# Two feed-forward layers: the first matrix of each in Strassen's 2x2 block scheme (7 block products instead of 8)

## Chip, cores and metric

One core of a Trainium2 chip runs one program. The metric is the device time of one execution in microseconds, as the median of runs. TensorE multiplies, VectorE and ScalarE read and write both SBUF and PSUM, GpSimd (POOL) works on SBUF, and SyncE (SP) issues the transfers.

## The reference

Attention over 2 x 8 heads of 576 tokens with 64 columns, with rotary tables, gives `x` of 1152 tokens and 512 columns. Then two feed-forward layers follow, and float32 accuracy is asked for:

```python
p = domain_probs / (domain_probs.sum(-1, keepdims=True) + 1e-09)
for e in range(4):                       # w1[e] 512 x 1024, w2[e] 1024 x 512, float32
    h = np.maximum(x @ w1[e], 0.0)
    out += p[:, e:e + 1] * (h @ w2[e])
x = out
h = x @ w_in                             # 512 x 2048, float64
g = np.maximum(0.01 * h, h)
return (g @ w_out).astype(np.float32)    # 2048 x 512, float64
```

## The kernel before

To keep float32 accuracy every operand of a matmul is held as two rounded halves, a high one and a low one, and each product is three matmuls (high x low, high x high, low x high).

The two layers are cut into 12 units of 512 hidden columns: units 0 to 7 are halves of the four experts, units 8 to 11 are quarters of the second layer. A unit's first matrix (`stage1`, L554 to L559, tile `ph`) works in blocks of 512, 384 and 256 tokens; for each block and each of four tiles of 128 hidden columns, 12 matmuls (four row chunks, three each) accumulate in one PSUM bank. Then ScalarE writes the rectified high half and VectorE the low half of `h` (L566, L570; in the second layer four steps, L578 to L584, the last on GpSimd). The second matrix (`stage2`, L586, tile `py`) takes 12 matmuls of 512 columns for each tile of 128 tokens, and VectorE adds them into `acc` (L605 or L609). For units 0 to 2 the first 512 tokens were already done during the attention part in half units (`half_1`, `half_2`), so these units have only the other 640 tokens.

The weights of a unit are loaded by SP into `raw` (8 buffers) and split into `w`, two buffers for each matrix: high half on GpSimd or ScalarE (L262, L260), low half `raw - high` on GpSimd (L519). The float64 weights of the second layer are narrowed as integers while they are needed, in eight steps a chunk (`split64`, L521 to L548). Between the layers every tile of `acc` is transposed on TensorE (L620) and split into `xT` (L623, L627).

The order on all engines is written out ahead by `Plan` (L77): each task has one or several possible engines with estimated durations, a rank, and the tasks that it must follow; a list scheduler gives each engine, whenever it is free in the plan, the ready task of lowest rank. What it writes is the program's fixed order, and each engine works its queue in that order.

```python
            t, e = best

            _, _, i, us = min((x for x in ready[e] if x[0] <= t), key=lambda x: (x[0], x[2]) if e == "DMA" else x[1:3])
            free[e] = t + us
            done[i] = e
```

Of the kernel before, what the change touches and what calls it, by code (L numbers as in the profile page):

```python
# [29 lines left out]
AHEAD = 3  # L30
FH = FU // 2
# [29 lines left out]
BLOCKS = [(0, 512), (512, 384), (896, 256)]  # L61
# [92 lines left out]
def attention_then_two_ffns(ctx, tc, xqk, vp, rope, dprob, w1, w2, w_in, w_out, out):  # L154
# [314 lines left out]
    RAW, W, ACC, HT, PH, PY, G, CV, TURN = ({} for _ in range(9))  # L469
    SEQ = [(u, b) for u in range(NU) for b in range(u < AHEAD, 3)]  # L470

    def unit_weights(u, which):
        if u < 2 * E:
            e, half = divmod(u, 2)
            a = (w1[e][:, half * FU:(half + 1) * FU], w2[e][half * FU:(half + 1) * FU, :])[which]
        else:
            j = u - 2 * E
            a = (w_in[:, j * FU:(j + 1) * FU], w_out[j * FU:(j + 1) * FU, :])[which].bitcast(I32)
        return a.rearrange("(c p) f -> p c f", p=P)

    def load_w(u, which, j, raw_p):

        src = unit_weights(u, which)
        if u < 2 * E:
            raw = RAW[u, which, j] = raw_p[0].tile([P, 2, raw_p[2]], F32, tag=raw_p[1], name=f"raw{u}_{which}_{j}")
            sp.dma_start(raw[:, :, :FU], src[:, 2 * j:2 * j + 2])
        else:
            raw = RAW[u, which, j] = raw_p[0].tile([P, FU, 2], I32, tag=raw_p[1], name=f"raw{u}_{which}_{j}")
            sp.dma_start(raw.rearrange("p f w -> p (f w)"), src[:, j])

    def w_place(u, which):
        if (u, which) not in W:
            pool_w = w2_p if which else w1_p
            W[u, which] = pool_w.tile([P, NC, 2, FU], F32R, tag=f"w{which}", name=f"w{which}_{u}")

    def add_split(plan, u, which, loaded, waits, rank, cv=None):

        res = []
        for c in range(NC):
            if u < 2 * E:  # L500

                hi = plan.add(lambda e, c=c: split_hi(e, u, which, c), [("POOL", 0.6, 0)] + [("ACT", 0.6, 0)] * (u == 0), loaded[c // 2:c // 2 + 1] + waits, rank + .1 * c)
                res.append(plan.add(lambda e, c=c: split_lo(e, u, which, c), [("POOL", 1.23, 0)] + [("DVE", 0.9, 0)] * (u == 0), [hi], rank + .1 * c))
                continue
            t = loaded[c:c + 1] + cv.new()
            for k, (e, us) in enumerate((("DVE", 0.85), ("DVE", 1.0), ("ACT", 0.65), ("ACT", 0.65), ("POOL", 1.4), ("DVE", 1.0), ("ACT", 0.62), ("POOL", 1.38))):
                t = [plan.add(lambda e, c=c, k=k: split64(u, which, c, k), [(e, us, 0)], t + (waits if k == 6 else []), rank + .1 * c)]
            cv.use(-1, t[0])
            res += t
        return res  # L510

    def split_hi(e, u, which, c):
        w_place(u, which)
        w, raw = W[u, which][:, c], RAW[u, which, c // 2][:, c % 2, :FU]
        rounded(e, w[:, 0], raw)

    def split_lo(e, u, which, c):
        w, raw = W[u, which][:, c], RAW[u, which, c // 2][:, c % 2, :FU]
        eng[e].tensor_tensor(out=w[:, 1], in0=raw, in1=f32(w[:, 0]), op=ALU.subtract)  # L519

    def split64(u, which, c, k):  # L521

        raw = RAW[u, which, c]
        low, high = raw[:, :, 0], raw[:, :, 1]
        if k == 0:
            CV[u, which, c] = [cv_p.tile([P, FU], d, tag=g, name=f"{g}{u}_{which}_{c}") for g, d in (("t", I32), ("r", I32), ("sq", F32))]
        t, r, sq = CV[u, which, c]
        if k == 0:

            dve.tensor_scalar(t, high, 3, 0x3FFFFFFF, op0=ALU.logical_shift_left, op1=ALU.bitwise_and)  # L530
        elif k == 1:
            dve.scalar_tensor_tensor(out=t, in0=high, scalar=-0x40000000, in1=t, op0=ALU.bitwise_and, op1=ALU.bitwise_or)  # L532
        elif k == 2:

            act.activation(r, low.bitcast(U32), AF.Copy, scale=2.0 ** -29)
        elif k == 3:
            act.activation(sq, high.bitcast(F32), AF.Square)
        elif k == 4:
            pool.tensor_tensor(out=t, in0=t, in1=r, op=ALU.add)  # L539
        elif k == 5:  # L540

            dve.scalar_tensor_tensor(out=f32(t), in0=sq, scalar=MIN_HIGH ** 2, in1=f32(t), op0=ALU.is_ge, op1=ALU.mult)
        elif k == 6:
            w_place(u, which)
            act.activation(W[u, which][:, c, 0], f32(t), AF.Copy)  # L545
        else:
            w = W[u, which][:, c]
            pool.tensor_tensor(out=w[:, 1], in0=f32(t), in1=f32(w[:, 0]), op=ALU.subtract)  # L548

    def h_place(k):  # L550
        u, blk = SEQ[k]
        HT[u, blk] = h_p.tile([P, 2, FU // P, 512], F32R, tag="h", name=f"h{u}_{blk}")

    def stage1(u, blk, f, ps, cs=range(NC)):  # L554
        w, x = W[u, 0], xT[blk]
        fs = slice(f * P, (f + 1) * P)
        for c in cs:
            for k, (l, r) in enumerate(((0, 1), (0, 0), (1, 0))):
                pe.matmul(ps, lhsT=w[:, c, l, fs], rhs=x[:, r, c], start=(c, k) == (0, 0), stop=(c, k) == (NC - 1, 2))  # L559

    def h_parts(u, blk, f):
        n = BLOCKS[blk][1]
        return HT[u, blk][:, 0, f, :n], HT[u, blk][:, 1, f, :n]

    def h_relu_hi(u, blk, f, ps):
        act.activation(h_parts(u, blk, f)[0], ps, AF.Relu)  # L566

    def h_relu_lo(u, blk, f, ps):
        hi, lo = h_parts(u, blk, f)
        dve.scalar_tensor_tensor(out=lo, in0=ps, scalar=0.0, in1=f32(hi), op0=ALU.max, op1=ALU.subtract)  # L570

    def h_leaky(u, blk, f, ps, k):
        hi, lo = h_parts(u, blk, f)
        if k == 0:
            G[u, blk, f] = g_p.tile([P, 512], F32, tag="g", name=f"g{u}_{blk}_{f}")[:, :BLOCKS[blk][1]]
        g = G[u, blk, f]
        if k == 0:
            act.activation(g, ps, AF.Copy, scale=0.01)  # L578
        elif k == 1:
            dve.tensor_tensor(out=g, in0=ps, in1=g, op=ALU.max)  # L580
        elif k == 2:
            act.activation(hi, g, AF.Copy)  # L582
        else:
            pool.tensor_tensor(out=lo, in0=g, in1=f32(hi), op=ALU.subtract)  # L584

    def stage2(u, blk, i, cs):  # L586
        w, ht = W[u, 1][:, :, :, cs], HT[u, blk]
        ps = PY[u, blk, i, cs.start] = ps_y.tile([P, cs.stop - cs.start], F32, tag="y", name=f"py{u}_{blk}_{i}_{cs.start}")
        ts_ = slice(i * P, (i + 1) * P)
        ops = []  # L590
        for f in range(FU // P):
            ops += [(ht[:, 0, f, ts_], w[:, f, 1]), (ht[:, 0, f, ts_], w[:, f, 0]), (ht[:, 1, f, ts_], w[:, f, 0])]
        products(ps, ops)

    def accumulate(u, blk, i, cs):
        ps = PY[u, blk, i, cs.start]
        t = BLOCKS[blk][0] // P + i
# [13 lines left out]
    def store(blk, i, cs):  # L611
        t = BLOCKS[blk][0] // P + i
        sp.dma_start(out[t * P:(t + 1) * P, cs], ACC[t][:, cs])

    def turn(blk, i):

        t = BLOCKS[blk][0] // P + i
        TURN[blk, i] = ps_h.tile([P, NC, P], F32, tag="h", name=f"tr{t}")
        for c in range(NC):
            pe.transpose(TURN[blk, i][:, c], ACC[t][:, c * P:(c + 1) * P], ident)  # L620

    def turn_hi(blk, i):
        act.activation(xT[blk][:, 0, :, i * P:(i + 1) * P], TURN[blk, i], AF.Copy)  # L623

    def turn_lo(blk, i):
        s = slice(i * P, (i + 1) * P)
        dve.tensor_tensor(out=xT[blk][:, 1, :, s], in0=TURN[blk, i], in1=f32(xT[blk][:, 0, :, s]), op=ALU.subtract)  # L627
# [68 lines left out]
    with tc.manual_schedule():  # L696
# [237 lines left out]
        def weights(u, which, rank):  # L934
# [8 lines left out]
            for c, t in enumerate(split[u, which]):  # L943
                rings["raw"].use(raws[c if u >= 2 * E else c // 2], t)
# [111 lines left out]
```

## Time and profile before

| | us |
|---|---|
| median of 3 runs | 777.24 (776.08 to 779.43) |
| the profiled execution's span | 775.8 |
| TensorE busy in it | 751.8 |
| VectorE, ScalarE, GpSimd busy | 431.3, 306.3, 406.8 |
| attention part | 0 to about 239 |
| feed-forward layers | about 239 to 773 |

For the profiled execution no time is given but its span, from the first to the last instruction. In a row of the trace, `x48` is a number of instructions, `<-` joins what is written to what is read, and `[5.39 <-PE ph L559]` is idle time before an instruction and what ended it.

### The profile page before, as it was taken

To read this page: it belongs to the slowest core of one execution; us is meant where nothing else is said; L and a number is where in the kernel's file an instruction comes from. 1 tells how busy PE (TensorE), PEld (TensorE's weight loads), DVE (VectorE), ACT (ScalarE), POOL (GpSimd) and SP (SyncE) were. 2 spreads that over 40 slices of the span, in tenths; PEclk is the share of its full clock that TensorE was granted. 3 is DMA by queue.
4 is the path that set the end of the run, shared out by engine and by line. 5 is a ranking of instruction groups with operands and counts; after the bars stand their busy time and mean duration, and the time that the engine had idled before them with its cause. 6 is when DMAs were issued, how large, how long until landed. Compare 5 with 4: busy or idle time off the path is not lost.

```text
span 775.8 us, 11040 instructions
## 1 busy us (share of the span) xinstructions
PE 751.8 (97%) x4204; PEld 663.8 (86%) x4204; DVE 431.3 (56%) x693; ACT 306.3 (39%) x693; POOL 406.8 (52%) x420
## 2 busy tenths in 40 slices
PE   6789899999999999999999999999999999999998
PEld 6678778888889989898898888988888889888897
DVE  7998978777765222222224222267678886662222
ACT  5588885666643101110112101043356454551221
POOL 7877967565268673433215331244158777682221
PEclk9999999999999999999999999999999999999999
DMA  8665645544064421211013100123112321000011
GB/s 261 170 200 156 156 105 145 155 117 122 1 245 144 129 82 55 82 55 45 11 54 109 56 28 27 55 58 107 55 55 81 108 84 55 0 1 1 1 55 68
DMA packets 31844, 67.70 MB, mean 87 GB/s; under 512 B 3888, under 2 KB 8752, under 8 KB 31792
## 3 DMA queue, kind: packets, MB, share of 16 engines
q1 hardware_dynamic: 30976, 66.22, 28.9%
q10 hardware_dynamic: 816, 0.79, 0.3%
q8 instruction: 33, 0.54, 0.3%
q14 instruction: 19, 0.16, 0.1%
HBM read 52.25 MB, written 2.36 MB: 70 GB/s over the span
## 4 chain that ended last, share of the span: by engine, by line
PE 87%; DVE 5%; POOL 3%; DMA 2%; ACT 1%; issue 1%; SPq 0%; ACTq 0%; POOLq 0%; DVEq 0%
PE ph L559 34%; PE py L464 34%; PE hp L662 4%; PE hy L464 4%; PE s L304 3%; PE o L464 3%; PE t L387 2%; DVE pt L416 1%; DVE nm L321 1%; DMA x<-in_xqk_dram 1%; DMA tab<-in_rope_dram 1%; POOL x L224 1%; POOL hw L655 1%; DVE x L221 1%; ACT p L331 1%
## 5 line engine op out<-in xcount | busy, mean ns | idle before, releaser
L559 PE MATMUL ph<-xT,w 128*128 128x384 f32 (+2 forms) x1584 | 273.2, 331 | 0.0
L559 PEld LDWEIGHTS ph<-xT,w 128*128 128x128 f32 x1584 | 252.2, 189 | 18.6
L464 PE MATMUL py<-w,h 128*128 128x512 f32 (+1 forms) x1164 | 267.9, 388 | 0.0
L464 PEld LDWEIGHTS py<-w,h 128*128 128x128 f32 x1164 | 215.9, 188 | 43.3
L566 ACT ACTIVATE h<-ph 128x384 fp32r<-128x384 f32 (+2 forms) x84 | 40.0, 476 | 248.7 <-PE ph L559 248.7
L262 POOL TENSOR_SCALAR w<-raw 128x512 fp32r<-128x512 f32 x58 | 35.6, 635 | 134.6 <-PE py L464 81.7
L570 DVE SCALAR_TENSOR_TENSOR h<-ph,h 128x384 fp32r<-128x384 f32 (+2 forms) x84 | 45.2, 539 | 108.5 <-ACT h L566 108.5
L605 DVE SCALAR_TENSOR_TENSOR acc<-py,prob,acc 128x512 f32<-128x512 f32 x55 | 41.3, 750 | 87.4 <-PE py L464 87.4
L584 POOL TENSOR_TENSOR h<-g,h 128x512 fp32r<-128x512 f32 (+2 forms) x48 | 52.7, 1101 | 60.4 <-ACT h L582 39.6
L519 POOL TENSOR_TENSOR w<-raw,w 128x512 fp32r<-128x512 f32 x62 | 79.5, 1307 | 4.5 <-ACT w L260 4.5
L548 POOL TENSOR_TENSOR w<-t,w 128x512 fp32r<-128x512 f32 x32 | 43.8, 1379 | 56.8 <-ACT w L545 55.5
L416 DVE TENSOR_TENSOR pt<-t,pt 128x384 fp32r<-128x384 f32 (+2 forms) x128 | 60.1, 491 | 8.7 <-ACT pt L412 7.2
L412 ACT ACTIVATE pt<-t 128x384 fp32r<-128x384 f32 (+2 forms) x128 | 53.4, 439 | 26.0 <-PE t L387 22.9
L304 PE MATMUL s<-stk 128*128 128x288 f32 x288 | 53.2, 314 | 8.1 <-ACT p L331 5.4
L331 ACT ACTIVATE p<-s,nm 128x576 f32<-128x576 f32 x72 | 53.3, 740 | 12.8 <-DVE nm L321 12.2
L539 POOL TENSOR_TENSOR t<-t,r 128x512 int32<-128x512 int32 x32 | 45.8, 1432 | 22.8 <-DVE t L532 13.4
L321 DVE TENSOR_REDUCE nm<-s 128x1 f32<-128x576 f32 x72 | 53.6, 749 | 3.9 <-PE s L304 3.1
L387 PE MATMUL t<-ident,p 128*128 128x128 f32 x288 | 45.5, 276 | 9.5 <-ACT p L331 3.7
L304 PEld LDWEIGHTS s<-stk 128*128 128x128 f32 x288 | 41.6, 192 | 12.3 <-ACT p L331 7.7
L387 PEld LDWEIGHTS t<-ident,p 128*128 128x128 f32 x288 | 34.4, 140 | 16.4 <-ACT p L331 4.7
L578 ACT ACTIVATE g<-ph 128x512 f32<-128x512 f32 (+2 forms) x48 | 23.4, 487 | 56.2 <-PE ph L559 54.7
L580 DVE TENSOR_TENSOR g<-ph,g 128x512 f32<-128x512 f32 (+2 forms) x48 | 26.6, 554 | 33.2 <-ACT g L578 32.9
(100 smaller groups left out, 864.8 us busy)
## 6 DMA issues: line engine op xcount, KB each, us to landing
raw<-in_w_dram SPq DMA_DIRECT2D x32, 512.0 KB, 3.7
raw<-in_w_in_dram SPq DMA_DIRECT2D x16, 512.0 KB, 3.8
raw<-in_w_out_dram SPq DMA_DIRECT2D x16, 512.0 KB, 3.6
x<-in_xqk_dram SPq DMA_DIRECT2D x14, 576.0 KB, 6.5
stk<-hl SPq DMA_DIRECT2D x28, 288.0 KB, 5.4
hraw<-in_w_dram SPq DMA_DIRECT2D x12, 512.0 KB, 3.8
stk<-hl SPq DMA_DIRECT2D x28, 144.0 KB, 3.5
v<-in_vp_dram SPq DMA_DIRECT2D x8, 288.0 KB, 4.7
```

What stands on the lines that cost most here:

```text
L304: pe.matmul(sc[:, c, :HS], lhsT=l, rhs=r[:, c * HS:(c + 1) * HS], start=(k == 0), stop=(k == len(ops) - 1))
L321: dve.tensor_reduce(out=NM[n], in_=SC[n][:, :, :HS], axis=AX.XY, op=ALU.max, negate=True)
L331: act.activation(PP[p, i][:, h].rearrange("p (c k) -> p c k", c=2), SC[n][:, :, :HS], AF.Exp, bias=NM[n], accum_out=SM[p][:, col:col + 1])
L387: pe.transpose(t[:, j], flat[:, b * P:(b + 1) * P], ident)
L412: act.activation(hi, src, AF.Copy)
L416: dve.tensor_tensor(out=lo, in0=src, in1=f32(hi), op=ALU.subtract)
L464: pe.matmul(ps, lhsT=l, rhs=r, start=(k == 0), stop=(k == len(ops) - 1))
L519: eng[e].tensor_tensor(out=w[:, 1], in0=raw, in1=f32(w[:, 0]), op=ALU.subtract)
L539: pool.tensor_tensor(out=t, in0=t, in1=r, op=ALU.add)
L559: pe.matmul(ps, lhsT=w[:, c, l, fs], rhs=x[:, r, c], start=(c, k) == (0, 0), stop=(c, k) == (NC - 1, 2))
L570: dve.scalar_tensor_tensor(out=lo, in0=ps, scalar=0.0, in1=f32(hi), op0=ALU.max, op1=ALU.subtract)
L584: pool.tensor_tensor(out=lo, in0=g, in1=f32(hi), op=ALU.subtract)
```

## The change

The first matrix of units 1 to 11 is computed as 2 x 2 blocks: the weights' 512 x 512 into four, `x`'s rows and a token block's two halves into four. Seven products of sums and differences give the four blocks of the result. The token blocks are now 512 and 640, so that a product's matmuls have 256 or 320 columns. Unit 0 uses eight products as before (`stage1_whole`). A quad is one token block and one of two tiles of 128 columns in each half; its seven products of six matmuls yield four output tiles.

The partial sums are not formed outside: product 1 goes into a bank, ScalarE copies it into a second bank, on which product 6 accumulates; this again is copied into a third, on which product 3 accumulates; after product 7 the second is copied into a fourth for product 4. Product 5 is copied to SBUF and VectorE adds it into two of the banks. The products of two quads are interleaved.

The weights' sums S1 to S4 and x's differences T1 to T4 are formed in four SBUF tiles `tmp` and split into halves. Each of the seven first-matrix weight tiles and four second-matrix weight tiles has one buffer now; `raw` has three. The eight PSUM banks become four `start` and four `seeded` ones. In the plan the last second-matrix tile of a unit is ranked later by `HOLD`.

The float64 weights are narrowed to float32 during units 0 to 7 (`converted`, 32 chunks with two sets of buffers), stored to DRAM and loaded again as ordinary float32 weights.

```diff
-BLOCKS = [(0, 512), (512, 384), (896, 256)]
+HOLD = 3.5
+BLOCKS = [(0, 512), (512, 640)]
+CUTS = [512, 896]
+HALVES = [n // 2 for _, n in BLOCKS]
...
+    A11, A12, A22, S1, S2, S3, S4 = range(7)
+    B11, B21, B22, T1, T2, T3, T4 = range(7)
+    PRODUCTS = {1: (A11, B11), 2: (A12, B21), 3: (S4, B22), 4: (A22, T4), 5: (S1, T1), 6: (S2, T2), 7: (S3, T3)}
...
+    def product(g, j, m, bank, first):
+        a, b = PRODUCTS[m]
+        out, fs = bank[:, :HALVES[g]], slice(j * P, (j + 1) * P)
+        for c in range(2):
+            for k, (l, r) in enumerate(((0, 1), (0, 0), (1, 0))):
+                pe.matmul(out, lhsT=W1[a][:, l, c, fs], rhs=x_of(g, b, r, c), start=first and (c, k) == (0, 0), stop=(c, k) == (1, 2), skip_group_check=True)
...
-        raw_p, w1_p, w2_p, h_p, g_p, cv_p, acc_p = (opened2(n, b) for n, b in (
-            ("raw", 8), ("w1", 2), ("w2", 2), ("h", 2), ("g", 3), ("cv", 2), ("acc", 1)))
-        ps_h, ps_y = opened2("ps_h", 4, space=PSUM), opened2("ps_y", 4, space=PSUM)
+        raw = [raw_p.tile([P, 2, FU], F32, name=f"raw{i}") for i in range(3)]
+        W1 = [w1_p.tile([P, 2, 2, 2 * P], F32R, name=f"w1_{i}") for i in range(7)]
+        W2 = [w2_p.tile([P, 2, FU], F32R, name=f"w2_{i}") for i in range(NC)]
+        tmp = [tmp_p.tile([P, 2, max(HALVES)], F32, name=f"tmp{i}") for i in range(4)]
+        sb = [bank_p.tile([P, 512], F32, name=f"start{i}") for i in range(4)]
+        db = [bank_p.tile([P, 512], F32, name=f"seeded{i}") for i in range(4)]
+        narrow = [[dram_p.tile([DM, FU], F32, name=f"narrow{j}_{w}") for w in range(2)] for j in range(F2 // FU)]
...
+        def halves(name, hi, lo, x, n, rank, reads, slot, first=None, second=None):
+            do(lambda e: rounded(e, hi, x), round_(n, **(first or {"POOL": 0, "ACT": 2})), rank, reads, [slot])
+            do(sub(lo, x, f32(hi)), pair(n, **(second or {"POOL": 0, "DVE": 3})), rank, list(reads) + [slot], [slot])
...
+            sums = {S1: (0, a[1, 0], a[1, 1], ALU.add, [slot[1, 0], slot[1, 1]]), S2: (1, t[0], a[0, 0], ALU.subtract, [("tmp", 0), slot[0, 0]]),
+                    S3: (2, a[0, 0], a[1, 0], ALU.subtract, [slot[0, 0], slot[1, 0]]), S4: (3, a[0, 1], t[1], ALU.subtract, [slot[0, 1], ("tmp", 1)])}
...
+                    do(sub(t[o], x, y, f), pair(n, POOL=0, DVE=0.5), due + i, reads, [("tmp", o)])
+                    op(w, t[o], [("tmp", o)], due + i + .2)
...
+        def converted(i, due):
+            moved(lambda: sp.dma_start(raw_.rearrange("p f w -> p (f w)"), wide_weights(j, which)[:, c]), 512, due - 12, (), [w, ("low", k)])
...
+            d = moved(lambda: sp.dma_start(narrow[j][which][c * P:(c + 1) * P, :], f32(t)), 256, due, [("rest", k)], [("narrow_", i)])
...
+        def x_differences(g, due):
+            for i, o, x, y in ((T1, (0, 0), (0, 1), (0, 0)), (T3, (0, 1), (1, 1), (0, 1)), (T2, (1, 1), (1, 1), (0, 0)), (T4, (1, 0), (1, 0), (1, 1))):
...
+                do(sub(t[o], t[x], t[y]), pair(2 * n, DVE=0, POOL=0), due, slots, [("tmp", 2 * o[0] + o[1])])
+                halves(f"x{i}", x_block(g, i, 0), x_block(g, i, 1), t[o], 2 * n, due, [("tmp", 2 * o[0] + o[1])], ("x", g, i), {"ACT": 0, "POOL": 0}, {"DVE": 0, "POOL": 0})
...
+            seq, state = [(0, 1), (0, 5)], {}
+            for q in range(len(quads)):
+                more = q + 1 < len(quads)
+                seq += [(q, 6), (q, 2)] + [(q + 1, 1)] * more + [(q, 7), (q, 3)] + [(q + 1, 5)] * more + [(q, 4)]
...
+                def seeded(name, of, due):
+                    i = {"b": q % 2, "c": 2, "d": 3}[name]
+                    st[name] = db[i], ("seed", i)
+                    src, s = st[of]
+                    do(lambda e, o=db[i][:, :n], x=src[:, :n]: act.activation(o, x, AF.Copy), on(n, ACT=0), due, [s], [("seed", i)])
...
+                on_ = {1: 1, 5: 5, 2: 1, 6: "b", 7: "b", 3: "c", 4: "d"}[m]
...
+                if m == 1:
+                    seeded("b", 1, now)
...
+                elif m == 6:
+                    seeded("c", "b", now)
...
+                elif m == 7:
+                    seeded("d", "b", now)
+                    add_fifth("b", now + 1)
+                    hidden(u, g, 2 + j, 1, b, s, now + 2)
+                elif m == 3:
+                    add_fifth("c", now + 1)
...
+                upto = convs if u == 2 * E - 1 else int(convs * (T + st2) / 300)
```

## Rows read from the trace of the kernel before

**Rows 1.** The page, parts 1 and 2: TensorE's busy time, and its granted clock in 40 slices
```profile
PE 751.8 (97%) x4204; PEld 663.8 (86%) x4204; DVE 431.3 (56%) x693; ACT 306.3 (39%) x693; POOL 406.8 (52%) x420
...
PEclk9999999999999999999999999999999999999999
```

**Rows 2.** The chain of waits from 239 us: start us, us, engine, tile, line, matmuls
```profile
239.35 14.09 PE ph L559 x96
...
416.22 10.88 PE ph L559 x48
427.10 5.44 PE py L464 x24
432.54 8.34 PE ph L559 x48
440.88 10.92 PE py L464 x48
451.80 5.75 PE ph L559 x48
457.56 8.19 PE py L464 x36
...
758.82 13.79 PE py L464 x72
```

**Rows 3.** Windows of units 0-2, 5, 9: us, PE, PEld, DVE, ACT, POOL, clock, DMA
```profile
239.35:317.16 77.81, 77.81 (x445) 71.57 (x445) 23.77 (x39) 10.52 (x24) 53.69 (x58) 1.00 0.34 107
416.22:465.74 49.52, 49.52 (x253) 43.38 (x253) 17.67 (x27) 8.15 (x16) 18.18 (x18) 1.00 0.21 64
...
618.42:667.95 49.53, 49.53 (x254) 43.39 (x253) 37.85 (x46) 24.63 (x48) 37.21 (x30) 1.00 0.21 65
```

**Rows 4.** Groups by shape from 239 us on ScalarE, VectorE, GpSimd: busy us, mean ns
```profile
L578 ACT ACTIVATE g<-ph 128x256 f32<-128x256 f32 x16 | 6.1, 384 | 26.1 <-PE ph L559 24.8
...
L570 DVE SCALAR_TENSOR_TENSOR h<-ph,h 128x256 fp32r<-128x256 f32 x32 | 13.6, 425 | 31.9 <-ACT h L566 31.9
...
L519 POOL TENSOR_TENSOR w<-raw,w 128x512 fp32r<-128x512 f32 x58 | 74.3, 1305 | 0.0
L539 POOL TENSOR_TENSOR t<-t,r 128x512 int32<-128x512 int32 x32 | 45.8, 1432 | 22.8 <-DVE t L532 13.4 <-ACT r L535 9.3
...
L262 POOL TENSOR_SCALAR w<-raw 128x512 fp32r<-128x512 f32 x56 | 34.4, 635 | 134.6 <-PE py L464 81.7 <-PE ph L559 52.9
...
L584 POOL TENSOR_TENSOR h<-g,h 128x256 fp32r<-128x256 f32 x16 | 12.5, 781 | 27.0 <-PE ph L559 18.0 <-ACT h L582 9.0
```

**Rows 5.** Timeline of GpSimd and VectorE in unit 9: start us, us
```profile
622.38 1.30 POOL L548 TENSOR_TENSOR w<-t,w 128x512 fp32r<-128x512 f32 x1 [1.39 <-ACT w L545]
622.42 1.80 DVE L542 SCALAR_TENSOR_TENSOR t<-sq,t 128x512 f32<-128x512 f32 x1
...
623.61 1.76 POOL L584 TENSOR_TENSOR h<-g,h 128x512 fp32r<-128x512 f32 x1
```

**Rows 6.** VectorE's three conversion operations: duration ns min/median/max
```profile
L542 DVE SCALAR_TENSOR_TENSOR t<-sq,t x32: 675/978/1801, 422.9 to 696.0; 128x512 f32<-128x512 f32 x32
...
L532 DVE SCALAR_TENSOR_TENSOR t<-raw,t x32: 675/818/1670, 417.4 to 689.7; 128x512 int32<-128x512 int32 x32
...
L530 DVE TENSOR_SCALAR t<-raw x32: 410/1200/1529, 416.9 to 688.8; 128x512 int32<-128x512 int32 x32
```

**Rows 7.** The chain of waits at the turn between the layers
```profile
526.15 10.88 PE py L464 x48
537.47 2.75 PE py L464 x12
```

**Rows 8.** Timeline of ScalarE in unit 5: start us, us
```profile
419.47 0.66 ACT L535 ACTIVATE r<-raw 128x512 int32<-128x512 uint32 x1
420.02 0.68 ACT L537 ACTIVATE sq<-raw 128x512 f32<-128x512 f32 x1
```

**Rows 9.** The page, part 6: KB of one transfer, us to landing
```profile
raw<-in_w_dram SPq DMA_DIRECT2D x32, 512.0 KB, 3.7
```

More of the change, by code (lines that the diff above doesn't have):

```diff
@@ L491, in w_place @@
[L491 to L498, printed above, removed]
-        for c in range(NC):
[L500 to L548, printed above, removed]
@@ L565, in h_relu_hi @@
[L565 to L584, printed above, removed]
@@ L609, in accumulate, with store @@
             dve.tensor_tensor(out=acc, in0=ps, in1=acc, op=ALU.add)
-    def store(blk, i, cs):
-        t = BLOCKS[blk][0] // P + i
+    def store(g, i, cs):
+        t = BLOCKS[g][0] // P + i
         sp.dma_start(out[t * P:(t + 1) * P, cs], ACC[t][:, cs])
[L615 to L627, printed above, removed]
     HW, HX, HP, HY = ({} for _ in range(4))
@@ L931, in attention_then_two_ffns @@
-        cv = Ring(2)
-        split, tiles = {}, {}
-        def weights(u, which, rank):
-            tiles[u, which], waits = fresh(f"w{which}")
-            loads = []
-            raws = []
-            for j in range(2 if u < 2 * E else NC):
-                r_t, r_w = fresh("raw")
-                raws.append(r_t)
-                loads.append(dma(lambda j=j: load_w(u, which, j, (raw_p, "raw", FU)), 512, r_w, rank - 3))
-            split[u, which] = add_split(plan, u, which, loads, waits, rank + (0.45 if u >= 2 * E else 0), cv)
-            for c, t in enumerate(split[u, which]):
-                rings["raw"].use(raws[c if u >= 2 * E else c // 2], t)
@@ new lines, in attention_then_two_ffns @@
+        tmp = [tmp_p.tile([P, 2, max(HALVES)], F32, name=f"tmp{i}") for i in range(4)]
+        xt = [{i: xt_p.tile([P, 2, 2, n], F32R, name=f"xt{g}_{i}") for i in (T1, T2, T4)} for g, n in enumerate(HALVES)]
+        HT = [h_p.tile([P, 2, FU // P, n], F32R, name=f"h{g}") for g, (_, n) in enumerate(BLOCKS)]
+        wide = [cv_p.tile([P, FU, 2], I32, name=f"wide{i}") for i in range(2)]
+        rest = [cv_p.tile([P, FU], I32, name=f"rest{i}") for i in range(2)]
+        sq = [cv_p.tile([P, FU], F32, name=f"sq{i}") for i in range(2)]
@@ new lines, in do @@
+        def do(fn, choices, rank, reads=(), writes=(), also=()):
+            after = set(also)
+            for s in reads:
+                after.update(written.get(s, ()))
+            for s in writes:
+                after.update(written.get(s, ()))
+                after.update(read.get(s, ()))
+            t = plan.add(fn, [(c[0], c[1], c[2] if len(c) > 2 else 0) for c in choices], after, rank)
+            for s in reads:
+                read.setdefault(s, []).append(t)
+            for s in writes:
+                written[s], read[s] = [t], []
+            return t
@@ new lines, in both, with moved, on @@
+        def both(*tasks, slot):
+            written[slot] = list(tasks)
+        def moved(fn, kb, rank, reads=(), writes=()):
+            t = do(lambda e: fn(), [("SP", 0.48)], rank, reads, writes)
+            d = plan.add(lambda e: None, [("DMA", kb / 260, 0)], [t], rank)
+            for s in reads:
+                read[s].append(d)
+            for s in writes:
+                written[s] = [d]
+            return d
+        def on(n, **more):
+            return [(e, {"ACT": 0.15 + n / 1200, "DVE": 0.13 + n / 960}[e], x) for e, x in more.items()]
@@ new lines, in attention_then_two_ffns, with turnof, load_w @@
+        spin = {"raw": 0, "start": 0, "g": 0, "fifth": 0}
+        def turnof(what, n):
+            spin[what] += 1
+            return (spin[what] - 1) % n
+        def load_w(u, which, rank):
+            rs = []
+            for j in range(2):
+                r = turnof("raw", len(raw))
+                rs.append(r)
+                src = unit_weights(u, which)[:, 2 * j:2 * j + 2]
+                moved(lambda r=r, src=src: sp.dma_start(raw[r], src), 512, rank - 12, [("narrow", u, which)], [("raw", r)])
+            return rs
@@ new lines, in stage1_whole @@
+        def stage1_whole(u, g, now):
+            n = HALVES[g]
+            banks = [(b, s) for b, s in zip(sb[:2] + db, [("start", 0), ("start", 1)] + [("seed", i) for i in range(4)])]
+            for i, (f, h) in enumerate([(f, h) for f in range(4) for h in range(2)]):
+                b, s = banks[(i + 2) % 6]
+                us = 12 * (n / 2400 + 0.0135)
+                x = [("x", g, v) for v in ((B11, B21), (T3, B22))[h]]
+                do(lambda e, f=f, h=h, b=b: whole(g, f, h, b), [("PE", us)], now, [("w1", A_OF[f // 2, k]) for k in range(2)] + x, [s])
+                now += us
+                hidden(u, g, f, h, b, s, now + 1)
+            return now
@@ new lines, in turned, with go @@
+        def turned(g, i, due):
+            n, t = HALVES[g], BLOCKS[g][0] // P + i
+            k = turnof("start", len(sb))
+            b = sb[k].rearrange("p (c t) -> p c t", c=NC)
+            def go(e):
+                for c in range(NC):
+                    pe.transpose(b[:, c], ACC[t][:, c * P:(c + 1) * P], ident)
+            do(go, [("PE", 0.45)], due - .5, [("acc", g, i, 0)], [("start", k)])
+            at = 0
+            while at < P:
+                h, off = divmod(i * P + at, n)
+                step = min(P - at, n - off)
+                for kk in range(2):
+                    slot = ("tmp", 2 * kk + h)
+                    o, x = tmp[2 * kk + h][:, :, off:off + step], b[:, 2 * kk:2 * kk + 2, at:at + step]
+                    w = written.get(slot, []) if (g, slot) in filling else None
+                    c = do(lambda e, o=o, x=x: (act.copy if e == "ACT" else dve.tensor_copy)(o, x), on(2 * step, ACT=0, DVE=0.2), due, [("start", k)], [] if w is not None else [slot])
+                    if w is not None:
+                        written[slot] = w + [c]
+                    filling.add((g, slot))
+                at += step
```

284 lines of the change are left out of this document (189 added, 95 removed).

## Prediction

> **What bounds the kernel now.** I read the page first. TensorE is busy 97% of the span at the full clock level (2.4 GHz) all the way [rows 1]. The chain of waits then says in which work: from 239.35 us on it is TensorE alone, groups of `ph` (the first matrix, L559) and `py` (the second, L464) that follow each other with no wait in an ordinary unit [rows 2]. In the windows TensorE is busy for all of 49.52 us of unit 5 and all of 49.53 us of a unit of the second layer, while VectorE, ScalarE and GpSimd have work for 8 to 38 us of it [rows 3]. So in the two feed-forward layers (239 to 773 us of 775.8) every matmul taken away shortens the kernel, as long as the other engines keep feeding TensorE.
>
> **What is removed.** The columns set the price: 48 matmuls of 512, 384 and 256 columns take 10.88, 8.34 and 5.75 us, so 226.7, 173.8 and 119.8 ns each [rows 2]. Weight loads of 128 columns stay hidden even at 256 columns, since that step lies on the same line as the others. The new pieces have 256 and 320 columns: 119.8 ns, and 146.8 ns as the middle of 256 and 384.
>
> - An ordinary unit (3 to 11, nine of them): before 10.88 + 8.34 + 5.75 = 24.97 us for the first matrix. After: for each block two quads of 7 products of 6 matmuls (a quad yields four output tiles), 84 x 119.8 + 84 x 146.8 ns = 10.06 + 12.33 = 22.39. Saved 2.58, times nine 23.2 us.
> - Units 1 and 2 (rest of the tokens only): before 8.34 + 5.75 = 14.09 [rows 2], after 12.33. Saved 3.5 us together.
> - Unit 0 multiplies the plain way: 96 x 146.8 ns = 14.09, nothing saved. The second matrix keeps its 512 columns.
>
> Sum: 26.7 us off TensorE, the most that the change can give. If nothing else moved, the span would be 775.8 - 26.7 = 749.1.
>
> **What is added beside TensorE.** Each quad (there are 40: two in each of units 1 and 2, four in each of nine units) needs three seed copies and one copy of the fifth product on ScalarE and two additions on VectorE. A 256-column ScalarE operation from PSUM takes 384 ns, a VectorE one 425 ns [rows 4]. That is about 1.6 us and 0.9 us in a quad of 7 x 0.72 = 5.03 us. With the four outputs of the second layer ScalarE has 12 operations, 4.6 us of 5.03 if none overlapped; but two in a row start 0.55 us apart where one takes 0.66 [rows 8], so nearer 3.8. The cover of each copy: the first seed lies under the fifth product (0.72 us against 0.38), the seed for the third under the second product and the next first one (1.44 us), and the held-back last tile of the second matrix lies at each unit's start. A copy behind one other ScalarE operation of 0.60 is late by about 0.3 us. If all are covered the cost is nothing; if one in each quad is late it is 40 x 0.3 = 12 us. I take 1.5 us, since ScalarE is busy 8.15 of 49.52 us in the first layer now [rows 3] and the seeds have early ranks.
>
> **The weights' sums and x's differences.** Here lies the doubt. Each unit's first matrix now needs four sums and seven splits, the second four splits: 15 two-operand operations of 512 columns between SBUF tiles (8 before), 1.31 us on GpSimd each [rows 4], or 0.68 us on VectorE when it is left alone (the shortest of the 32 in [rows 6]). The schedule lets both engines take them. But the rows say that they can't work at once. At 622.38 GpSimd starts 1.30 us of a two-operand operation; VectorE starts one of its own 0.04 us later and takes 1.80 us instead of 0.68, to 624.22, half a microsecond beyond GpSimd's end; GpSimd's next then takes 1.76 [rows 5]. Over 32 such VectorE operations the time goes from 675 to 1801 ns [rows 6]. So I count one shared resource on which both add up. The operations that read PSUM (the 425 ns ones) don't show it.
>
> The first three units, whose TensorE time is 14.09 + 2 x 12.33 + 3 x 13.63 = 79.6 us after the change, must take:
> - 45 operations of 512 columns for weights (33 for the first matrices of units 1 to 3, 12 for the second of 0 to 2),
> - 12 of 512 and 12 of 640 columns for x's sums, differences and splits of the two blocks,
> - 9 conversions of float64 due by then (the code spreads 32 over 300 us of its plan, and unit 2 ends at 91), each 1.43 us on GpSimd [rows 4] and 0.41 + 0.68 + 0.68 us on VectorE [rows 6]: 3.2 us, 28.8 in all; before the change these lay in the last third.
>
> Lower bound, all on VectorE undisturbed: 57 x 0.68 + 12 x 0.84 + 28.8 = 77.7 us: it just fits, no stall. Upper bound, three in five on GpSimd: 57 x 1.06 + 12 x 1.32 + 28.8 = 104.9, and some ten roundings on GpSimd at 0.64 [rows 4] make 111.3: 31.7 us too much. Now, of the same three units GpSimd is busy 53.69 of 77.81 and VectorE, mostly on PSUM, 23.77 [rows 3]. The conversions can wait: an ordinary unit has 15 x 1.06 + 5 x 3.2 = 32 us for 46.9. If they all gave way, 82.5 us remain for 79.6, a stall of 3. They don't wholly: engines take their queues in order, and an engine with nothing better to do is given a conversion early. Behind a late conversion on VectorE stand the additions to PSUM and the accumulations, and for them TensorE waits. Between 3 and 32 I take 10 us.
>
> The Trainium skill (SBUF — State Buffer, "Who interferes with whom") says the same more strictly: a VectorE instruction with two SBUF inputs uses a read interface that it shares with GpSimd, and whoever has it holds it for the whole instruction. Taken to the letter, with no conversion giving way, its sum is the upper bound, and it is the second rival below. The trace agrees in [rows 5], where 1.80 us is 1.30 of waiting and 0.5 of work.
>
> **The turn between the layers.** x is transposed into four temporaries which the weights' sums use too, then split and differenced: 11 operations for each block, 11 x 1.06 + 11 x 1.32 = 26.2 us, with unit 8's weights (15.9) and the second layer's 16 low halves on GpSimd at 0.78 us for 256 columns [rows 4], so about 0.9 on the mean: 14. That is 56 us for the 51 us of unit 7's second matrix with its transposes (28.5) and unit 8's first (22.4). Before, TensorE lost 0.44 us at each of five places there; the first: 526.15 + 10.88 = 537.03, and the next group starts at 537.47 [rows 7]. Added: 0 to 10 us; I take 3, since the second block's x is needed only 10 us into unit 8.
>
> **Hidden.** The conversions' 32 wide loads move forward, and 32 narrow stores and 16 re-loads of half a megabyte are new on SP's queue. A store waits for VectorE's last multiplication, and behind it stand weight loads; these are ranked 12 us ahead and land in 3.7 us [rows 9], so a late store of some 5 us stays covered. If the cover were gone, each late pair of loads would cost those 3.7 us. W1 and W2 are single now, but each is refilled in the other matrix's 22 to 25 us (in 12 to 14 in the first three units, counted above). The second layer loses its conversions, where GpSimd and VectorE had 37 us of 49.53 [rows 3]; nothing is gained by that, since TensorE didn't wait there. The attention part keeps its order and its 239 us.
>
> **Sum.** 775.8 - 26.7 + 1.5 + 10 + 3 = 763.6 of span. The median of the runs, 777.2, lies 1.4 above the profiled span, so 765.0 us.
>
> **Rivals.**
> 1. *Nearly all of it arrives.* The conversions give way and VectorE takes most of the sums; 2 us of stalls in all: 775.8 - 26.7 + 2 + 1.4 = 752.5. For it: the busiest unit now has 37.21 and 37.85 us on the two engines and TensorE waits for neither [rows 3]. Against: the first three units are packed more tightly than that. 0.17.
> 2. *The shared SBUF interface becomes the bound (slower).* In units 0 to 3 GpSimd and VectorE each run behind the order planned for them as if they were independent, and TensorE waits for weights, x and PSUM additions: the full 31.7 us, and with 1.5 and 3: 775.8 - 26.7 + 36.2 + 1.4 = 786.7. For it: [rows 5, 6]. Against: the deferrable 28.8 us. It decides the sign once all stalls exceed 26.7, and slower by 0.5% once they exceed 30.6. 0.23.
> 3. *The seeds bind.* ScalarE's copy is late once in each quad: 12 us rather than 1.5, with the rest as forecast 775.5, no change. For it: TensorE can't go on to the sixth product without the first seed. Against: ScalarE's low load. 0.12.
>
> My forecast has 0.48, with its own range 756 to 773. A difference under 0.5% (3.9 us) can't be told from none here. Faster: 0.47 + 0.17 + 0.02 = 0.66; same: 0.01 + 0.09 + 0.02 = 0.12; slower 0.22. The range for 8 in 10 cuts a third off the first rival and half off the second: 752 to 784.
>
> **What would show it.** In the changed kernel's windows, TensorE's matmul groups of an ordinary unit should take 22.4 us for the first matrix, and its gaps should lie between 239 and 320 us and around the turn. There the two-operand VectorE operations should take over 1 us on the mean. If gaps come after the seed copies instead, in each quad, the third rival holds. If TensorE's gaps in the first three units exceed 25 us, the second. The prediction is wrong if 320-column products cost more than 147 ns each, or if waits appear in units 3 to 7.

## The result and the profile after

The changed kernel takes 785.9 us (median of four runs, 784.0 to 786.3) against 777.1 for the kernel before (four runs, 776.1 to 779.4). The ratio is 1.0102, with the interval 1.0083 to 1.0122. It is 1% slower, outside the range of 752 to 784 us and on the other side of my 765. The second rival had 786.7 us. The profiled execution took 783.96 us, with a span of 782.1.

The page of the kernel after, parts 1, 2 and 5 (in part 5: busy us, mean ns, idle before):

```profile
PE 734.7 (94%) x4396; PEld 658.2 (84%) x4396; DVE 552.9 (71%) x914; ACT 395.1 (51%) x964; POOL 458.2 (59%) x452
...
PEclk9999999999999999999999999999998999999999
...
L515 PE MATMUL seeded<-xT,w 128*128 128x320 f32 (+1 forms) x480 | 74.9, 307 | 12.5 <-ACT seeded L1042 12.5
```

Against [rows 1], TensorE's busy time fell by 17.1 us only, and its share from 97% to 94%. VectorE went from 431.3 to 552.9 us. TensorE now waits in the first matrix (L515), after seed copies.

First, where it works as forecast. The chain of waits of the kernel after, a unit of the second layer (start us, us):

```profile
663.06 19.07 PE start L467 x84
...
683.56 2.75 PE start L467 x12
...
704.62 2.75 PE start L467 x12
...
710.00 19.07 PE start L467 x84
```

From one group of 84 to the next is 46.94 us, where [rows 3] had 49.53: 2.59 us saved in a unit, forecast 2.58. Without the second matrix (19.07 + 2.75 + 2.75) the first takes 22.37 us, forecast 22.39.

The windows of the kernel after (us, then busy us of PE, PEld, DVE, ACT, POOL, granted clock, DMA share, GB/s): all of units 0 to 2, the second matrix of unit 0 among them, unit 3, units 4 to 7 as far as the turn, the turn, and a unit of the second layer:

```profile
239.35:341.24 101.89, 84.15 (x438) 73.93 (x439) 94.54 (x112) 45.14 (x93) 81.53 (x57) 0.97 0.49 148
...
260.68:273.21 12.53, 11.29 (x48) 9.04 (x49) 12.44 (x15) 4.52 (x8) 11.27 (x8) 1.00 0.66 198
...
341.24:388.34 47.10, 47.10 (x279) 42.81 (x278) 34.79 (x58) 23.91 (x53) 28.31 (x22) 1.00 0.51 155
388.34:554.14 165.80, 165.80 (x1010) 152.48 (x1009) 113.29 (x194) 72.94 (x172) 78.58 (x70) 1.00 0.37 117
554.14:616.12 61.98, 57.50 (x327) 50.82 (x326) 43.62 (x64) 29.89 (x76) 40.49 (x38) 0.94 0.10 35
616.12:663.06 46.94, 46.94 (x277) 42.66 (x277) 24.24 (x44) 21.23 (x56) 24.90 (x27) 1.00 0.14 46
```

TensorE has no gap in units 3 to 7 before the turn, nor in the second layer behind it (units 9 to 11). The whole loss lies in two places:

- **Units 0 to 2.** Without a stall, unit 3's first 256-column product would start at 239.35 + 79.6 - 2.7 (the second-matrix tile held behind it) = 316.3 us. It starts at 341.24, 24.9 us late. VectorE is busy for 94.54 of 101.89 us, in [rows 3] for 23.77 of 77.81; GpSimd for 81.53.
- **The turn.** From there to the end, the sum without stalls leaves 749.1 - 316.3 = 432.8 us, and it takes 440.9: 8.1 us late.

Together 33.0 us are lost of the 26.7 saved, which is the 6.3 us between the spans.

The timeline of TensorE in the kernel after, the gaps of over 3 us with undisturbed groups among them (start us, us, matmuls, idle before):

```profile
260.68 2.77 PE L467 MATMUL start<-w,h 128*128 128x512 f32 x11 [3.24 <-DVE h L1004]
...
276.83 1.04 PE L515 MATMUL start<-xt,w 128*128 128x320 f32 x6
277.71 1.04 PE L515 MATMUL seeded<-xt,w 128*128 128x320 f32 x6
...
288.98 2.77 PE L515 MATMUL seeded<-xT,w 128*128 128x320 f32 x12 [3.19 <-ACT seeded L1042]
...
316.04 1.92 PE L515 MATMUL seeded<-xt,w 128*128 128x320 f32 x12
...
324.31 3.46 PE L515 MATMUL seeded<-xT,w 128*128 128x320 f32 x12 [5.47 <-ACT seeded L1042]
...
599.15 2.93 PE L515 MATMUL seeded<-xT,w 128*128 128x256 f32 x12 [3.55 <-ACT seeded L1042]
```

These read like the third rival, a late seed. The timeline of the other engines ahead of the longest gap shows what the seed itself waited for:

```profile
314.80 1.27 POOL L909 TENSOR_TENSOR w<-raw,w 128x512 fp32r<-128x512 f32 x1
314.93 5.08 DVE L909 TENSOR_TENSOR w<-raw,w 128x512 fp32r<-128x512 f32 x3
...
316.03 1.75 POOL L978 TENSOR_TENSOR rest<-wide,rest 128x512 int32<-128x512 int32 x1
...
317.75 1.72 POOL L909 TENSOR_TENSOR w<-raw,w 128x512 fp32r<-128x512 f32 x1
...
319.94 0.68 DVE L979 SCALAR_TENSOR_TENSOR rest<-sq,rest 128x512 f32<-128x512 f32 x1
...
320.54 0.48 DVE L1004 SCALAR_TENSOR_TENSOR h<-start,h 128x320 fp32r<-128x320 f32 x1
320.70 0.68 ACT L975 ACTIVATE sq<-wide 128x512 f32<-128x512 f32 x1 [7.34 <-DVE rest L979]
...
323.84 0.42 ACT L1042 ACTIVATE seeded<-seeded 128x320 f32<-128x320 f32 x1 [0.29 <-DVE h L1004]
```

Three subtractions of weights on VectorE, 2.0 us by the 0.68 of [rows 6], take 5.08: each lies against one of GpSimd's three operations. Behind them and one conversion (L979) stand the reads of PSUM (L1004), behind those the seed copy, behind that TensorE. The queue is worked in order, so a wait for weights that are needed later becomes a wait of TensorE now. The delay also passes through ScalarE, which makes the seeds: it sat idle for 7.34 us, because at the head of its own queue stood a conversion's square (L975) that had to wait for L979 on VectorE.

The groups by shape of the kernel after, VectorE and GpSimd from 239 to 341 us:

```profile
L909 DVE TENSOR_TENSOR w<-raw,w 128x512 fp32r<-128x512 f32 x11 | 16.2, 1495 | 0.0
L977 DVE SCALAR_TENSOR_TENSOR wide<-wide 128x512 int32<-128x512 int32 x10 | 12.5, 1252 | 0.1
L976 DVE TENSOR_SCALAR wide<-wide 128x512 int32<-128x512 int32 x11 | 10.9, 988 | 1.1 <-ACT rest L974 1.1
L979 DVE SCALAR_TENSOR_TENSOR rest<-sq,rest 128x512 f32<-128x512 f32 x10 | 8.8, 879 | 1.2 <-POOL rest L978 1.2
...
L909 POOL TENSOR_TENSOR w<-raw,w 128x512 fp32r<-128x512 f32 x14 | 22.3, 1604 | 0.5 <-ACT w L263 0.5
L978 POOL TENSOR_TENSOR rest<-wide,rest 128x512 int32<-128x512 int32 x10 | 15.0, 1502 | 6.5 <-DVE wide L977 3.2 <-issue 2.1 <-ACT fifth L1062 1.1
```

By the shortest durations in [rows 6] (0.68, and 0.41 for L976) VectorE's four groups would take 11 x 0.68 + 10 x 0.68 + 11 x 0.41 + 10 x 0.68 = 25.6 us; they take 48.4. So 22.8 us of VectorE's time lie above the undisturbed durations; e2_one_input below shows that contact with GpSimd makes them. Ten conversions fell into these units; the forecast had nine.

### The profile page after: what moved, and what is told of

Read it like the earlier page. It is cut to its first block, busy times and chain, and to the rows that moved or that the text cites. A ratio compares the mean times of both kernels' runs of the same rounds, so it can differ in the third digit from the quotient of the medians.

```text
span 782.1 us, 12238 instructions
## 1 busy us (share of the span) xinstructions
PE 734.7 (94%) x4396; PEld 658.2 (84%) x4396; DVE 552.9 (71%) x914; ACT 395.1 (51%) x964; POOL 458.2 (59%) x452
## 4 chain that ended last, share of the span: by engine, by line
PE 72%; DVE 14%; POOL 5%; issue 3%; DMA 3%; ACT 2%; SPq 1%; POOLq 0%; ACTq 0%; DVEq 0%
PE start L467 30%; PE seeded L515 15%; PE start L515 10%; PE hy L467 4%; PE hp L588 4%; PE s L307 3%; PE o L467 3%; PE t L390 2%; DVE w L909 2%; DVE tmp L909 2%; DMA x<-in_xqk_dram 2%; DVE nm L324 1%; DVE pt L419 1%; POOL tmp L909 1%; DVE wide L977 1%
## 5 line engine op out<-in xcount | busy, mean ns | idle before, releaser
L467 PE MATMUL start<-w,h 128*128 128x512 f32 (+1 forms) x1164 | 269.8, 389 | 5.9 <-DVE h L1004 5.9
L467 PEld LDWEIGHTS start<-w,h 128*128 128x128 f32 x1164 | 215.1, 188 | 49.7 <-DVE h L1004 7.1
L515 PE MATMUL seeded<-xT,w 128*128 128x320 f32 (+1 forms) x480 | 74.9, 307 | 12.5 <-ACT seeded L1042 12.5
L515 PEld LDWEIGHTS seeded<-xT,w 128*128 128x128 f32 x480 | 70.3, 198 | 14.2 <-ACT seeded L1042 13.5
L515 PE MATMUL seeded<-xt,w 128*128 128x320 f32 (+1 forms) x480 | 74.7, 302 | 0.0
L515 PE MATMUL start<-xT,w 128*128 128x320 f32 (+1 forms) x480 | 73.4, 298 | 0.1
L515 PEld LDWEIGHTS seeded<-xt,w 128*128 128x128 f32 x480 | 69.6, 194 | 0.9 <-ACT seeded L1042 0.3
L515 PEld LDWEIGHTS start<-xT,w 128*128 128x128 f32 x480 | 67.5, 190 | 1.5 <-DVE g L1009 0.3
L909 POOL TENSOR_TENSOR h<-g,h 128x256 fp32r<-128x256 f32 (+1 forms) x64 | 55.2, 883 | 19.2 <-ACT h L1010 19.1
L909 DVE TENSOR_TENSOR w<-raw,w 128x512 fp32r<-128x512 f32 x46 | 51.2, 1142 | 7.4 <-ACT w L263 5.2
```

What stands on the lines that cost most here:

```text
L467: pe.matmul(ps, lhsT=l, rhs=r, start=(k == 0), stop=(k == len(ops) - 1))
L515: pe.matmul(out, lhsT=W1[a][:, l, c, fs], rhs=x_of(g, b, r, c), start=first and (c, k) == (0, 0), stop=(c, k) == (1, 2), skip_group_check= ...
L909: return lambda e: eng[e].tensor_tensor(out=o, in0=a, in1=b, op=op)
```

## The experiments

Three theories stood against each other. A: the SBUF interface that VectorE and GpSimd share is overbooked in units 0 to 2, and the queues, worked in order, carry the delay to TensorE. B: the single-buffered weight tiles and the four `tmp` tiles make a chain of dependences that is too long, whatever the engines do. C: the schedule gives VectorE too much work. e1_late, e2_one_input, e3_shared_plan and e4_both were timed together (the kernel before took 777.6 us there), the other four likewise (777.0).

In the table, "late" is measured as above: unit 3's start less 316.3, and from there to the end of the span less 432.8. Both are taken from the profiled execution, whose time differs from the median by up to 3.4 us (e6_one_engine).

| kernel | us, median (range) | ratio to before (95%) | unit 3 late | the rest late |
|---|---|---|---|---|
| after | 785.9 (784.0–786.3) | 1.0102 (1.0083–1.0122) | 24.9 | 8.1 |
| e1_late | 773.9 (773.2–776.7) | 0.9955 (0.9941–0.9968) | 7.8 | 18.0 |
| e1b_late | 773.0 (772.8–774.3) | 0.9953 (0.9937–0.9970) | 7.0 | 15.0 |
| e2_one_input | 755.3 (755.0–755.6) | 0.9712 (0.9693–0.9732) | 4.5 | 0.2 |
| e3_shared_plan | 766.3 (764.7–767.8) | 0.9860 (0.9843–0.9876) | 9.2 | 4.6 |
| e4_both | 762.4 (761.3–763.7) | 0.9804 (0.9789–0.9818) | 4.8 | 6.6 |
| e6_one_engine | 771.1 (767.8–772.2) | 0.9917 (0.9893–0.9941) | 11.4 | 5.5 |
| e7_start | 782.7 (780.4–785.8) | 1.0072 (1.0049–1.0095) | 21.6 | 8.6 |
| e5_candidate | 755.7 (755.3–758.0) | 0.9732 (0.9716–0.9748) | 0.7 | 4.0 |

**e1_late: no conversions in units 0 to 2.** They wait for unit 3's first task and spread over units 3 to 7.

```diff
-            if u < 2 * E:
-                upto = convs if u == 2 * E - 1 else int(convs * (T + st2) / 300)
+            if AHEAD <= u < 2 * E:
+                upto = convs * (u - AHEAD + 1) // (2 * E - AHEAD)
...
-                    converted(i, T + st2 * (i - done + 1) / max(1, upto - done))
+                    converted(i, T + st2 * (i - done + 1) / max(1, upto - done), [first])
```

> The changed kernel, but no float64 conversion starts before unit 3; the 32 are spread over units 3 to 7. Theory A (VectorE's and GpSimd's SBUF work shares one interface and is too much in units 0 to 2): 10 conversions of 3.2 us leave the first three units, the stall there falls from 24.9 us to about 6 or less, units 3 to 7 stay without a wait; about 767 us. Theory B (the single weight and x tiles are the limit: each split waits until TensorE has left its tile, however free the engines are): the stall stays, 784 us.

Measured 773.9, where theory A had about 767. Units 0 to 2 come near to what A says (7.8 us late for about 6), and the time isn't B's 784; but the rest is 18.0 us late, which A did not have. In this kernel two of ScalarE's copies at the turn changed places, so that a piece of the second block's transposed `x` overwrites one that is still being split; the amount of work is the same. e1b_late keeps them in order.

**e1b_late: the same, with the later pieces of a temporary behind its first.** Added to the edit of e1_late (the later kernels e5, e6 and e7 have this line too):

```diff
-... due, [("start", k)], [] if w is not None else [slot])
+... due, [("start", k)], [] if w is not None else [slot], w or ())
```

> The changed kernel, but no float64 conversion starts before unit 3 (the 32 are spread over units 3 to 7), and at the turn the later pieces of a transposed block follow its first piece into a temporary. Theory A (VectorE's and GpSimd's SBUF work shares one interface and is too much in units 0 to 2): the stall of the first three units, 24.9 us, falls to 4 to 8, but units 3 to 7 and the turn get more; 772 to 776 us. Theory B (the single weight and x tiles are the limit, however free the engines are): 784 us.

Measured 773.0. The forecast of the total was made with e1_late's time known; what it tests is B, which had 784. The windows of e1b_late, for the stretch that was units 0 to 2 in the kernel after (here unit 3 starts at 323.29) and for the turn:

```profile
239.35:341.24 101.89, 98.09 (x570) 88.64 (x570) 80.60 (x113) 41.82 (x92) 64.86 (x50) 1.00 0.31 102
540.00:616.00 76.00, 67.38 (x378) 58.72 (x377) 61.55 (x86) 37.67 (x90) 55.46 (x47) 0.98 0.22 72
```

Units 0 to 2 lose 7.0 us instead of 24.9: with the conversions in them 17.9 of these go. B falls here, since every weight and temporary tile is as single as before. But the rest loses 15.0 instead of 8.1: TensorE has 1.8 us of gaps between 341 and 540 us, and four conversions now fall between 540 and 616 us, where the kernel after has none (VectorE 61.55 us of 76, TensorE 67.38), beside x's differences and unit 8's weights. Of 17.9 us gained, 6.9 are given back.

**e2_one_input: the same order, no contact.** VectorE's operations of these layers that came into contact are each replaced by one that reads a single SBUF tile of the same size. That arithmetic (the low halves, sums and differences that fall to VectorE, and three steps of the conversion) is left out; the number of these operations and the planned order stay. Two things change besides: each replacement is followed by a read of its accumulator (82 ns), and an operand that is no longer read is no longer waited for or held.

```diff
-            return lambda e: eng[e].tensor_tensor(out=o, in0=a, in1=b, op=op)
+            return lambda e: alone(o, b) if e == "DVE" else eng[e].tensor_tensor(out=o, in0=a, in1=b, op=op)
+        def alone(o, x):
+            dve.tensor_scalar(o, x, 1.0, 0.0, op0=ALU.mult, op1=ALU.add, accum_out=total)
```

> The changed kernel with the same order of work, but VectorE's two-input operations between SBUF tiles (weights, x, conversion) read one input only and leave the arithmetic on the other out; so the number of operations stays and only the contact with GpSimd goes. Theory A: these VectorE operations fall from 0.9 to 1.6 us to about 0.7 each and GpSimd's two-input ones from 1.5 to 1.3, the first three units lose at most 6 us and the time is about 763 us. Theory B, or a plan that simply has too much work on VectorE whatever the interface: 780 to 786 us.

Measured 755.3, where A had about 763. The window of e2_one_input for the same stretch of time (unit 3 starts at 320.76 in it), and its groups by shape from 239 to 341 us:

```profile
239.35:341.24 101.89, 99.63 (x585) 90.58 (x584) 81.23 (x215) 59.80 (x127) 78.58 (x68) 1.00 0.58 180
```
```profile
L914 DVE TENSOR_SCALAR_CACHE_REDUCE wide<-wide 128x512 f32<-128x512 f32 x27 | 18.4, 683 | 2.4 <-ACT rest L979 1.7
L914 DVE TENSOR_SCALAR_CACHE_REDUCE w<-w 128x512 fp32r<-128x512 f32 x20 | 13.6, 682 | 1.3 <-ACT w L263 0.2
...
L909 POOL TENSOR_TENSOR w<-raw,w 128x512 fp32r<-128x512 f32 x17 | 21.9, 1298 | 3.8 <-ACT w L263 3.7
```

This is the plainest evidence for A. VectorE's operations last 683 ns with GpSimd at work for 78.58 of 101.89 us beside them; GpSimd's own fall from 1604 to 1298 ns. Up to the start of unit 3 the same ten conversions run as in the kernel after, and TensorE is busy for 79.15 of 81.41 us. 28.3 of the 33.0 us of stalls are gone with the contact. Too much work on VectorE whatever the interface, for which 780 to 786 us were expected, falls with that. B isn't settled by this run alone, since the operands that are no longer read take some dependences with them; e1b_late and e5_candidate, which read every operand, settle it.

**e3_shared_plan: the plan knows of the interface.** The list scheduler gets one more resource. Every GpSimd task and every VectorE task that came into contact occupies it, and starts only when it is free. The conversions are also costed at their undisturbed durations.

```diff
+        def begin(e, x):
+            return max(free.get(e, 0.0), x[0], free.get("shared", 0.0) if x[4] else 0.0)
...
-            _, _, i, us = min((x for x in ready[e] if x[0] <= t), key=...)
+            _, _, i, us, both = min((x for x in ready[e] if begin(e, x) <= t), key=...)
             free[e] = t + us
+            if both:
+                free["shared"] = t + us
```

> The changed kernel with an order of work planned with one more resource that GpSimd's operations and VectorE's two-input SBUF operations occupy together, the conversions costed at their undisturbed 0.42, 0.66, 0.66 and 1.3 us. Theory A: the demand stays, but PSUM work on VectorE no longer stands behind an operation that waits, and the conversions give way: the stall of the first three units falls to 8 to 15 us, about 772 us. Theory B: no change, 784 us.

Measured 766.3. No work is taken away and none forbidden in any unit; only the order and the choice of engines differ. The conversions give way in part: seven start before unit 3 instead of ten. The stalls fall from 33.0 to 13.8 us, and 766.3 is better than the 772 that A had. So the 10 us that I forecast for units 0 to 2 is about what a plan that knows the resource pays (9.2); the plan that was run doesn't.

**e4_both: that plan, with the late conversions of e1_late.**

> The changed kernel with both: conversions from unit 3 on, and the order planned with the shared resource. Theory A: the first three units lose 3 us or less and the turn 3 to 8: 755 to 762 us, faster than both kernels. Theory B: 782 us or more.

Measured 762.4, just above A's range: units 0 to 2 are 4.8 us late where 3 or less was expected. That is less than with either edit alone (7.8 and 9.2). At the turn e4_both loses 2 us more than e3_shared_plan; four conversions start after 540 us in it and none in e3_shared_plan.

**e6_one_engine: give VectorE more.** Planned as the kernel after, but a two-operand sum or split that either engine may take goes to VectorE alone; GpSimd keeps roundings, the conversions' additions and the second layer's low halves.

```diff
+            more = {e: x for e, x in more.items() if e == "DVE" or len(more) == 1}
```

> The changed kernel, but every two-operand sum and split of weights and x that both engines could take goes to VectorE alone; GpSimd keeps the conversions' additions, the roundings and the second layer's low halves. Theory A: the operations fall to about 0.7 to 0.9 us each; VectorE then has 49 us of them, 18 of conversions and 27 of PSUM work for the 80 us of the first three units, a stall of some 15 there and 3 at the turn: 768 to 774 us, faster than the changed kernel by over 10. Rival C (VectorE, busy for 77 of 81 us there, simply has too much work, and GpSimd helps it): more work on VectorE makes it slower, 792 us or more.

Measured 771.1, inside A's 768 to 774. The groups by shape of e6_one_engine from 239 to 341 us:

```profile
L910 DVE TENSOR_TENSOR w<-raw,w 128x512 fp32r<-128x512 f32 x29 | 20.9, 750 | 0.0
...
L979 POOL TENSOR_TENSOR rest<-wide,rest 128x512 int32<-128x512 int32 x9 | 15.8, 1757 | 39.6 <-DVE wide L978 11.4 <-ACT w L263 10.9 <-issue 9.4
```

In the same stretch 29 operations in place of 11 take 20.9 us in place of 16.2. C falls: VectorE gets more work, and unit 3 starts 13.5 us earlier. Some of the gain may come from the new plan, which starts eight conversions before unit 3 instead of ten. Theory A gives the reason for the gain: an operation holds the interface for 0.68 us on VectorE and for 1.3 on GpSimd.

**e7_start: x's sums behind unit 0's weights.** The first block's sums for Strassen aren't needed in unit 0, and stood ahead of its weights.

```diff
-                x_sums(1, 12)
+                x_sums(1, 12, [t for i in A_OF.values() for t in written["w1", i]])
```

> The changed kernel, but the first sums of x may only start behind the split of unit 0's weights (which GpSimd can do while it waits for x, as before the change). Theory A: VectorE's last 0.25 us operations of the attention part no longer wait for GpSimd, TensorE reaches unit 0 1.2 to 3 us earlier; 782 to 785 us, the rest of the stall stays. Theory B: the same 1 to 3 us.

Measured 782.7. Unit 0 starts at 237.87 us instead of 240.75, and unit 3 starts 3.3 us earlier (21.6 late), though the granted clock over the stretch is lower (0.92 against 0.97). The rest stays. It is a small part of the loss by itself, and A and B had the same for it, so it tells nothing between them.

**e5_candidate: the plan of e3_shared_plan, the edit of e7_start, and conversions over units 3 to 6, so that they end before the turn.**

```diff
+                upto = min(convs, convs * (u - AHEAD + 1) // (2 * E - AHEAD - 1))
```

> Planned with the shared resource, conversions spread over units 3 to 6 only, x's first sums behind the split of unit 0's weights. Theory A: first three units 1 us, turn 3 us or less: 756 to 760 us. Theory B: no faster than the run with late conversions and the shared plan (762.4).

Measured 755.7, faster than both kernels and slightly below A's 756 to 760. The window of e5_candidate for the same stretch (unit 3 starts at 316.98) and the waits of TensorE (us in total, times, longest):

```profile
239.35:341.24 101.89, 101.21 (x595) 91.99 (x594) 83.42 (x125) 51.22 (x112) 52.66 (x41) 1.00 0.34 109
```
```profile
PE seeded L520 <- ACT seeded L1047: 1.6, 2, 1.1
PE start L1117 <- DVE acc L550: 0.8, 1, 0.8
PE start L472 <- DVE h L1009: 0.5, 1, 0.5
```

The computation is that of the kernel after, with the same single tiles and every operand read. Units 0 to 2 are 0.7 us late, so B's chain of dependences isn't what held them. The turn still costs 4.0, where 3 or less was expected; no run takes these apart. Of the 26.7 us that Strassen's scheme takes off TensorE, 753.8 against 775.8 leaves 22.0 us of span.

## Why the prediction was wrong, point by point

- **TensorE's saving: right.** 2.59 us in an ordinary unit against 2.58; 320-column matmuls take 0.88 us for six, 146.7 ns against 146.8.
- **The first three units, "Between 3 and 32 I take 10 us": the step that failed.** It measured 24.9 us. The mechanism was named, and the size lay inside the bounds; the choice between them was wrong. I let most conversions give way ("The conversions can wait"). They didn't: the plan reserves no shared resource, so both engines seem free to it, and it placed ten conversions in this stretch. e1b_late prices them at 17.9 of the 24.9. With them gone 7.0 us are left where I had 3. About 3 of these belong to the start of unit 0, which had no term in my sum ("The attention part keeps its order and its 239 us"): in the kernel after it begins 1.4 us late and then waits 1.8 us for its weights, and e7_start takes both away. The upper bound was good: the three units took 79.6 + 24.9 = 104.5 us, and 111.3 was the sum with every operation on one resource.
- **What was in the 24.9.** Idle time 101.89 - 84.15 = 17.7; unit 0's start 1.4 later than 239.35 (240.75), with the attention's last work in that time; about 3 by the clock (0.97 on the mean of 101.89 us). The last 2.7 are not assigned.
- **The turn, 3 us: too small as well.** It measured 8.1, inside the 0 to 10. Idle time is 61.98 - 57.50 = 4.5, and the granted clock of 0.94 over 61.98 us makes 3.7 more. In e2_one_input 0.2 remain, so it was the same interface. My own count there, 56 us of work for 51, already said 5. The 0.44 us that I called lost "at each of five places" before the change were no waits; TensorE transposes a tile of `acc` there (L620), and no idle time stands before it. The timeline of the kernel before, at the first of them:

```profile
536.87 0.60 PE L620 MATMUL tr<-ident,acc 128*128 128x128 f32 x4
```

- **The seeds, 1.5 us: nothing where the kernel runs freely.** In units 3 to 7 and 9 to 11 no seed is late. The 12.5 us of waits on seed copies that the page shows (8.7 in units 0 to 2, 3.9 at the turn) are the stalls of these two places at their last link: in e2_one_input they fall to 0.2 us, the seeds themselves unchanged.
- **SP's queue and the single buffers: right.** No wait of TensorE is put down to a transfer, and B, which would have made the buffers guilty, fell.
- **The second rival** gave 786.7 us and was 0.8 from the median. Its account was right in kind: VectorE and GpSimd behind a plan that treats them as independent. It had 31.7 + 3 + 1.5 where 24.9, 8.1 and 0 were measured, so its total is nearer than its parts. That is partly luck: from the profiled execution's 783.96 us it is 2.7 away. In my own sum the three terms beside TensorE's saving, 10, 3 and 1.5, came to 33.0 us instead of 14.5.

The rule of the Trainium skill that stood beside it (SBUF — State Buffer, "Who interferes with whom") agrees with the traces in both its halves: a VectorE instruction with two SBUF inputs contends with GpSimd and is held back for the other's instruction (1495 ns on the mean where 0.68 us is the work), and one with a single SBUF input, of the form that e2_one_input uses, isn't (683 ns). I had given the strict reading 0.23; its 111.3 us for the three units lie nearer to the measured 104.5 than my 89.6.

## What to carry to other kernels

Where a change trades matmuls for elementwise work, add up what VectorE does with SBUF operands and all that GpSimd does as one resource, for each stage by itself, and compare it with TensorE's time in that stage; shares over the whole span (71% and 59% here) hide it. If a list scheduler writes the order, give it that resource, and tie work that can wait to a later unit rather than trust a rank: together with e7_start's edit the two turned 785.9 us into 755.7 with the same computation. When TensorE waits for a short copy, follow the chain back through the in-order queue to the operation that took longer than its shortest, before blaming the copy.

## What the runs showed of the hardware

- **A gap can cost twice.** The windows of the kernel after, from the groups that followed gaps of 3.19, 5.47 and 3.55 us:

```profile
288.98:291.55 2.57, 2.57 (x13) 2.57 (x13) 2.57 (x5) 2.57 (x6) 1.68 (x2) 0.69 0.80 282
...
324.31:327.60 3.29, 3.29 (x12) 3.29 (x13) 3.26 (x5) 2.21 (x5) 1.28 (x1) 0.51 0.88 294
...
599.15:602.08 2.93, 2.93 (x13) 2.93 (x14) 2.93 (x4) 2.08 (x6) 2.13 (x3) 0.50 0.00 0
```

  The granted clock is 0.51 and 0.50 after the two longer gaps, the 1.2 GHz level, and 0.69 on the mean after the first. Twelve 320-column matmuls take 3.46 us instead of 1.92. After the 3.24 us gap at 260.68 the clock stayed at 1.00, so the length of the gap alone doesn't decide; what does, no run here tests.
- **An operation of one SBUF input was held up too.** L976 reads one tile and takes 0.41 us at best; it took 988 ns on the mean in units 0 to 2. Its replacement in e2_one_input, also of one input but 683 ns long and with an accumulator written, was not held up. What sets the two apart was not tried by itself. The Trainium skill has it in the section named above: a one-input form may take the shared pair in a faster mode, not when it also writes an accumulator; these two durations agree with that.
- **GpSimd is held up as well**: 1604 ns against 1298 for the same subtraction with and without contact.
